# The last 64 tokens of four batches as one seven-product block instead of two pairs of full products

## The chip, the cores and the metric

The kernel runs on one core of a Trainium2 chip. The metric is the device time of one execution in microseconds (us). Before the change three executions took 236.12, 236.27 and 237.04 us; the median is 236.27 us. A core has a matrix engine (TensorE, PE in the profile; its weight loads are PEld), a vector engine (VectorE, DVE), an activation engine (ScalarE, ACT), a general engine (GpSimd, POOL) and a queue engine (SyncE, SP). Each works through its own instructions in order. SBUF is the on-chip memory, PSUM the accumulator of TensorE with 8 banks.

## The reference

Eight batches of 576 tokens and 8 heads go through an attention with 32 memory slots per head, and then through a gated feed-forward block:

```python
a = exp(phi - max(phi)); a = a / sum(a)                 # per token, over 32 slots
k_m = einsum('bhsm,bhsd->bhmd', a, k)
v_m = einsum('bhsm,bhsd->bhmd', a, v)
attn = softmax(q @ k_m.T / 8)                           # 576 x 32 per head
x = attn @ v_m                                          # tokens x 512
h = silu(x @ w_gate) * (x @ w_val)                      # 4608 x 1536
out = h @ w_out                                         # 4608 x 512
```

Only the last line is touched by the change: h (tokens x 1536) times w_out (1536 x 512). All of k, v and the products are in bfloat16 with float32 accumulation.

## The kernel before

h of a batch lies as `hts[b, c]`, 128 x 4 x 576, for three chunks c of 512 of the 1536 columns; the contraction runs over 128-row blocks. Of the 576 tokens, 512 are multiplied with w_out by a scheme with seven block products in place of eight (2 x 2 blocks: tokens halves times contraction pairs on one side, contraction pairs times output halves on the other). It needs sums of blocks of h (`Ss`) and of w_out (`Ts`), and adds results in VectorE when they leave PSUM. One product has six units, one unit two matmuls of 128x256 (u = 0, 1):

```python
def products(b, by_hand):
    ...
    def product(home, lhs, rhs, after):
        def unit(k):
            c, m = k // 2, k % 2
            def run():
                fresh = k == 0 and home not in mine
                if fresh:
                    mine[home] = bank([128, 2, h], FP32, f"p_o{home}")
                    ...
                for u in range(2):
                    nc.tensor.matmul(mine[home][:, u], lhsT=lhs(c, m, u), rhs=rhs(c, m),
                                     start=fresh and u == 0, stop=(k == 5), ...)
                if k == 5:
                    ...
                    if after in now:
                        now[after]()          # p1, q6, p5: ScalarE copies; c11, c12, c22: VectorE adds; c21: copy
    ...
    if b + 1 == B:
        return first + six + five + seven + three + four, ops
    return first + five + six + three + seven + four, ops
```

The adds write output tiles of which there are three in turn, and each is stored by queue transfers:

```python
work = ctx.enter_context(tc.tile_pool(name="work", bufs=3))
...
def add(out, home, other, free=False):
    nc.vector.tensor_tensor(out=out, in0=mine[home], in1=mine[other], op=ALU.add)
    ...
def c22():
    t = tile_of("o2", (128, 2, DM), tag="to")
    add(t[:, :, hi], "s", "p5")               # reads bank "s" after product seven
...
def c12():
    t = mine["o1"]
    add(t[:, :, hi], "c", "q6", True)
    both("o1", 0, ...)                        # the stores of o1
def c21():
    copy("v" if box.get("end") else "a", mine["o2"][:, :, lo], mine["s"])
    ...                                       # the stores of o2
```

Banks are called by their home: "s" takes products 1, 6, 7 and 4 one after the other (all accumulate; between them p1, q6 and c22 read it), "c" takes 5 and 3 (p5 reads it between them), "a" takes the second half of `first`.

The block sums of h are made as each chunk is done: on GpSimd for chunks 0 and 1, on VectorE for chunk 2. The remaining 64 tokens of each batch are copied by GpSimd into `xs`, two batches side by side (2 x 64 = 128 tokens), and multiplied in full, 12 contraction blocks for each half of the 512 output columns:

```python
def chunk_done(b, c):
    ...
    sums(nc.vector if end else nc.gpsimd)      # end: c == 2
    ...                                        # ends(): GpSimd copies the last 64 tokens into xs[b // 2]

def out_rest(pair, half):                      # 6 units of 2 matmuls 128x256
    ...
    for jf in (2 * n, 2 * n + 1):
        nc.tensor.matmul(mine["p"], lhsT=xs[pair][:, jf]..., rhs=WO[jf][:, cols],
                         start=(jf == 0), stop=(jf == NJF - 1))
    if n == NJF // 2 - 1:
        copy("v" if box.get("end") else "a", t_o, mine["p"])
        ...                                    # and two stores
```

The order is written by hand. For each batch b from 2: the products of batch b-1 wait in a backlog of units. Scores and softmax of batch b come between 36 of them; then 24 gate/value slots (each two matmuls for the gate p_g, silu on ScalarE into t_sg, two matmuls for the value p_v, a multiply on VectorE into t_h), with the rest of the backlog as fillers, the key/value sums of the next batch after eight slots (they use sums of exp(phi) that GpSimd makes first), and the weights of the next batch (`u_three`, six banks, four copies on ScalarE and two on VectorE) after twenty:

```python
for b in range(2, B):
    ...
        backlog += out_rest(b // 2 - 1, b % 2)
        run(take(6))
    if b > 2:
        loads(b)                              # GpSimd issues the loads of batch b + 2
    for g in range(NG):
        scores(b, g)
    ...                                       # z_inv_v, norm (t_A), 30 more units of the backlog
    if b == 2:
        u_three(2)
        run(out_rest(0, 0))
        u_values(2)
        backlog = one[36:]
    g = gv_slots(b)
    beside = 0 if last else min(7, len(backlog))
    outs = [lambda: run(take(1)) for _ in range(len(backlog) - beside)]
    streams = [(g, 0, 24), (outs, 4, 24)]
    ...
        (kv_items(b + 1, lambda: (u_item(b, 2, "aava")(), run(take(2)))), KV, KV + 4),     # KV = 7
        ([lambda: (run(take(2)), u_three(b + 1), run(take(3)))], 19, 20),
    spread(*streams)
    ...
run_late()
run(take(6))
ops["p1"]()
run(out_rest(B // 2 - 1, 0))
box["end"] = True                             # from here ScalarE issues half of the stores
run(take(6))
ops["c11"]()
run(backlog)
run(out_rest(B // 2 - 1, 1))
```

Of the kernel before, what the change touches and what calls it, by code (L numbers as in the profile page):

```python
# [14 lines left out]
def kernel(  # L15
# [52 lines left out]
    box = {}  # L68
# [516 lines left out]
    def chunk_done(b, c):  # L585
# [26 lines left out]
        if end and b > 1:  # L612
            late.append(ends)
        else:
            ends()
        if (b, c) in beside_sums:
            beside_sums[b, c]()

# [4 lines left out]
    }  # L623

# [10 lines left out]
    def store(t_o, b, t0, count, row=0, cols=slice(0, 512), queues=None):  # L635

        if queues is None and box.get("end"):
            queues = nc.sync, nc.scalar
        for n, (r0, m, bb, jj, pp) in enumerate(token_segments(b, t0, count)):
            eng = queues[n % len(queues)] if queues else nc.sync  # L640
            eng.dma_start(out=out_r[bb, jj, pp:pp + m, cols], in_=t_o[row + r0:row + r0 + m])

    def out_rest(pair, half):

        h = DM // 2
        mine = {}
        cols = slice(h * half, h * half + h)

        def unit(n):
            def run():  # L650
                if n == 0:
                    mine["p"] = bank([128, h], FP32, "p_oo")
                for jf in (2 * n, 2 * n + 1):
                    nc.tensor.matmul(  # L654
                        mine["p"],
                        lhsT=xs[pair][:, jf].rearrange("p a t -> p (a t)"),
                        rhs=WO[jf][:, cols],
                        start=(jf == 0),
                        stop=(jf == NJF - 1),
                    )  # L660
                if n == NJF // 2 - 1:
                    t_o = work.tile([128, h], FP32, tag="to", name="t_o")
                    copy("v" if box.get("end") else "a", t_o, mine["p"])
                    done(mine["p"])
                    end = 2 * pair + 2 == B
                    for k in range(2):
                        store(
                            t_o, 2 * pair + k, S - 64, 64, 64 * k, cols,
                            ((nc.sync, nc.scalar)[k],) if end else None,
                        )  # L670

            return run

        return [unit(n) for n in range(NJF // 2)]

    def products(b, by_hand):
# [3 lines left out]
        lo, hi = slice(0, h), slice(h, DM)  # L680

        def A(e, n):
            return lambda c, m, u: hts[b, c][
# [3 lines left out]
        def Sx(n):  # L687
            return lambda c, m, u: Ss[b, c][:, n, m, 128 * u:128 * u + 128]
# [7 lines left out]
# [4 lines that stand above are left out]
                def run():  # L700
                    fresh = k == 0 and home not in mine
                    if fresh:
                        mine[home] = bank([128, 2, h], FP32, f"p_o{home}")
                        mine[home, "new"] = True
                    for u in range(2):
# [17 lines left out]
        def tile_of(name, shape=(128, 2, h), **kw):  # L723
# [14 lines left out]
        def both(name, t0, cols):  # L738
            for u in range(2):
                store(mine[name][:, u, cols], b, t0 + 128 * u, 128, cols=cols)  # L740

        def c11():
            t = tile_of("o1", (128, 2, DM), tag="to")
            add(t[:, :, lo], "a", "p1", True)
            if box.get("end"):
                both("o1", 0, lo)

        def c22():
            t = tile_of("o2", (128, 2, DM), tag="to")
            add(t[:, :, hi], "s", "p5")  # L750
            if box.get("end"):
                both("o2", 256, hi)

        def c12():
            t = mine["o1"]
            add(t[:, :, hi], "c", "q6", True)
            both("o1", 0, hi if box.get("end") else slice(0, DM))

        def c21():
            t = mine["o2"]  # L760
            copy("v" if box.get("end") else "a", t[:, :, lo], mine["s"])
            done(mine["s"])
            both("o2", 256, lo if box.get("end") else slice(0, DM))
# [12 lines left out]
        if b + 1 == B:  # L776
# [177 lines left out]
    for b in range(2, B):  # L954
# [25 lines left out]
        else:  # L980
            backlog += out_rest(b // 2 - 1, b % 2)
# [23 lines left out]
        if b == 2:  # L1005
            u_three(2)
            run(out_rest(0, 0))
            u_values(2)
            backlog = one[36:]
        g = gv_slots(b)  # L1010
        beside = 0 if last else min(7, len(backlog))
        outs = [lambda: run(take(1)) for _ in range(len(backlog) - beside)]
        streams = [(g, 0, 24), (outs, 4, 24)]
# [53 lines left out]
```

The softmax here doesn't subtract the row's maximum and nothing guards it: scores larger than these inputs give would overflow.

## Time and profile before

| | |
|---|---|
| median of 3 runs | 236.27 us |
| span of the profiled run | 234.5 us, TensorE clock 1.00 |
| TensorE busy | 225.9 us, 2847 matmuls |
| VectorE, ScalarE, GpSimd busy | 187.4, 172.5, 135.2 us |
| gate and value matmuls p_g, p_v (L514) | 768 of 128x288 |
| leftover matmuls p_oo (L654) | 96 of 128x256 |
| block sums of h on GpSimd (L601, L559) | 68 of 128x512, 1155 to 1186 ns each |
| copies of the last 64 tokens (L591) | 24 |

The page of the profile lists an engine's busy time, the chain of work that ended last, and groups of equal instructions: line, engine, operation, output<-inputs, shape, count | busy us, mean ns of one | idle time of the engine before them and what ended it. [...]the durations of matmuls overlap; the distance of their starts is what each costs. A timeline line gives start, duration, engine, line, instruction, count, and in brackets the idle time before it with its releaser. SPq and ACTq are the issues of transfers by those engines.

### The profile page before, as it was taken

The page shows a single profiled execution, that of the slowest core. Times are in us where ns is not written, and L with a number is a line of the kernel's source. Part 1 is how long each engine was busy: PE and PEld are TensorE (multiplying, and loading weights), DVE is VectorE, ACT ScalarE, POOL GpSimd, SP SyncE. Part 2 cuts the span into 40 slices and gives each one's busy share as a digit, 9 for nine tenths or more (in the row PEclk, how much of TensorE's full clock was granted, in tenths as well). Part 3 has the DMA queues.
Part 4 walks back from the last instruction along what each step waited for, and adds up shares of the span by engine and source line. Part 5 has one row for each costly group of instructions (what it writes and reads, how often), then busy time and mean ns, then how long its engine had stood idle before and what let it go on. Part 6 is the DMA issues. An engine that isn't in the chain of part 4 may idle for free.

```text
span 234.5 us, 7300 instructions
## 1 busy us (share of the span) xinstructions
PE 225.9 (96%) x2847; PEld 171.3 (73%) x2847; DVE 187.4 (80%) x417; ACT 172.5 (74%) x368; POOL 135.2 (58%) x171
## 2 busy tenths in 40 slices
PE   7998899999999999999999999999999999999992
PEld 2555466778887777887778777877788777878881
DVE  4157699999979697998799878988799879987621
ACT  2758888988447888977898779968897789677310
POOL 8532426999099159654992399267916493029400
PEclk9999999999999999999999999999999999999999
DMA  6999999999974999899559964999313721122134
GB/s 211 205 205 207 198 208 206 228 238 248 207 169 97 252 216 158 166 247 232 137 80 252 214 110 106 225 226 142 110 25 81 132 89 27 31 62 89 33 92 126
DMA packets 42914, 36.84 MB, mean 157 GB/s; under 512 B 15488, under 2 KB 38528, under 8 KB 42880
## 3 DMA queue, kind: packets, MB, share of 16 engines
q0 software_dynamic: 21440, 22.42, 55.0%
q1 hardware_dynamic: 20176, 12.79, 25.8%
q10 hardware_dynamic: 1264, 1.18, 1.6%
q8 instruction: 22, 0.36, 0.6%
q14 instruction: 12, 0.10, 0.1%
HBM read 42.47 MB, written 9.44 MB: 221 GB/s over the span
## 4 chain that ended last, share of the span: by engine, by line
PE 82%; DMA 8%; POOL 4%; DVE 3%; issue 1%; ACT 0%; DVEq 0%; POOLq 0%
PE p_g L514 20%; PE p_v L514 19%; PE p_os L706 16%; PE p_oc L706 8%; DMA t_kv<-in_v_dram 8%; PE p_u L471 5%; PE p_oo L654 5%; PE p_oa L706 4%; PE p_kv L235 2%; POOL t_es L217 1%; POOL t_q L108 1%; PE p_g L400 1%; POOL t_kv L98 1%; DVE t_lz L443 1%; DVE t_z L434 1%
## 5 line engine op out<-in xcount | busy, mean ns | idle before, releaser
L537 DVE TENSOR_TENSOR t_h<-t_sg,p_v 128x288 bf16<-128x288 bf16 x192 | 83.1, 452 | 15.6 <-PE p_v L514 7.6
L514 PEld LDWEIGHTS <-t_U 128*128 128x128 bf16 x768 | 73.7, 98 | 21.7 <-issue 2.9
L531 ACT ACTIVATE t_sg<-p_g 128x288 bf16<-128x288 f32 x192 | 74.5, 423 | 15.9 <-PE p_g L514 9.1
L514 PE MATMUL p_g<-t_A,t_U 128*128 128x288 bf16 x384 | 77.2, 286 | 0.0
L514 PE MATMUL p_v<-t_A,t_U 128*128 128x288 bf16 x384 | 77.0, 286 | 0.0
L706 PEld LDWEIGHTS <-t_S 128*128 128x128 bf16 x384 | 37.4, 98 | 4.5 <-issue 0.2
L601 POOL TENSOR_TENSOR t_S<-t_h 128x512 bf16<-128x512 bf16 x17 | 19.7, 1156 | 35.2 <-DVE t_h L537 35.2
L491 ACT CAST t_U<-p_u 128x512 bf16<-128x512 f32 x53 | 28.0, 608 | 8.9 <-PE p_u L471 8.9
L706 PEld LDWEIGHTS <-t_h 128*128 128x128 bf16 x288 | 27.3, 98 | 7.8 <-issue 4.0
L706 PE MATMUL p_os<-t_T,t_S 128*128 128x256 bf16 x192 | 23.7, 273 | 0.0
L559 POOL TENSOR_TENSOR t_S<-t_S,t_h 128x512 bf16<-128x512 bf16 x17 | 19.6, 1155 | 1.3
L559 POOL TENSOR_TENSOR t_S<-t_h,t_S 128x512 bf16<-128x512 bf16 x17 | 20.1, 1186 | 0.0
L559 POOL TENSOR_TENSOR t_S<-t_h 128x512 bf16<-128x512 bf16 x17 | 19.6, 1155 | 0.0
L471 PE MATMUL p_u<-W,t_kT 64*32 64x512 bf16 (+1 forms) x416 | 15.9, 363 | 0.1
L706 PE MATMUL p_os<-t_T,t_h 128*128 128x256 bf16 x96 | 15.6, 273 | 0.0
L827 PE MATMUL p_warm<-bones 128*128 128x512 bf16 (+2 forms) x43 | 12.9, 427 | 1.7 <-DVE bones L850 1.7
L451 DVE TENSOR_TENSOR t_A<-t_E,t_lz 128x576 bf16<-128x576 bf16 x16 | 13.4, 840 | 0.9 <-ACT t_lz L427 0.3
L654 PE MATMUL p_oo<-WO,t_x 128*128 128x256 bf16 x96 | 14.0, 273 | 0.0
L495 DVE CAST t_U<-p_u 128x512 bf16<-128x512 f32 x19 | 12.4, 683 | 1.6 <-PE p_u L471 1.6
L215 POOL COPY t_mark<-t_A 1x1 bf16<-1x1 bf16 x4 | 0.7, 182 | 20.3 <-DVE t_A L451 20.3
L706 PE MATMUL p_oc<-t_T,t_S 128*128 128x256 bf16 x96 | 12.0, 273 | 0.0
L706 PE MATMUL p_oa<-WO,t_h 128*128 128x256 bf16 x96 | 11.8, 273 | 0.0
(93 smaller groups left out, 309.9 us busy)
## 6 DMA issues: line engine op xcount, KB each, us to landing
t_kv<-in_k_dram POOLq DMA_DIRECT2D x8, 576.0 KB, 10.1
t_kv<-in_v_dram POOLq DMA_DIRECT2D x8, 576.0 KB, 14.4
out_dram<-t_o SPq DMA_DIRECT2D x21, 192.0 KB, 2.6
t_phi<-in_phi_dram POOLq DMA_DIRECT2D x6, 576.0 KB, 7.9
t_q<-in_q_dram POOLq DMA_DIRECT2D x5, 576.0 KB, 7.4
out_dram<-t_o SPq DMA_DIRECT2D x37, 64.0 KB, 2.0
out_dram<-t_o SPq DMA_DIRECT2D x14, 128.0 KB, 5.8
t_q<-in_q_dram POOLq DMA_DIRECT2D x6, 288.0 KB, 11.3
```

Of the source, the lines that this page charges most:

```text
L451: nc.vector.tensor_tensor(out=a, in0=es.pop((b, g)), in1=lzs.pop((b, g)), op=ALU.mult)
L471: nc.tensor.matmul(p[g][32 * i:32 * i + 32, o:o + n], lhsT=kTs[b][64 * g:64 * g + 64, 2, 32 * i:32 * i + 32], rhs=w_part(w, c, i, g, halve ...
L491: nc.scalar.copy(out=t, in_=p)
L495: nc.vector.tensor_copy(out=t, in_=p)
L514: nc.tensor.matmul(p[:, 0:HALF], lhsT=Us[b, c, g][:, o // 2, which, 128 * (o % 2):128 * (o % 2 + 1)], rhs=atts[b, g][:, r], start=(g == 0) ...
L531: nc.scalar.activation(out=sg, in_=gate[:, 0:HALF], func=AF.Silu)
L537: nc.vector.tensor_tensor(out=dst, in0=sg, in1=val[:, 0:HALF], op=ALU.mult)
L559: eng.tensor_tensor(out=out, in0=x, in1=y, op=ALU.subtract)
L601: eng.tensor_tensor(out=t[:, 0], in0=A21, in1=A22, op=ALU.add)
L654: nc.tensor.matmul(mine["p"], lhsT=xs[pair][:, jf].rearrange("p a t -> p (a t)"), rhs=WO[jf][:, cols], start=(jf == 0), stop=(jf == NJF - 1),)
L706: nc.tensor.matmul(mine[home][:, u], lhsT=lhs(c, m, u), rhs=rhs(c, m), start=fresh and u == 0, stop=(k == 5), skip_group_check=u == 1 or n ...
L827: nc.tensor.matmul(p[:, 0:128 * a], lhsT=bones, rhs=x.to_broadcast([128, a, 128]) if a > 1 else bones, start=True, stop=True,)
```

## The change

Four batches have 4 x 64 = 256 leftover tokens: with the pair of batches as token halves, the same seven-product scheme fits, with a single matmul of 128x256 per unit in place of two. `products` gets a parameter `quad` for it: U = 1, the h blocks come from `xs[2 * quad]` and `xs[2 * quad + 1]`, and the block sums are made by GpSimd in `quad_sums`, four instructions of 128x256 for each chunk (one of them writes over a block in place). Quad 0 (batches 0 to 3) runs within the first six slots of batch 4. Quad 1 (batches 4 to 7) runs its first 12 units among the slots of batch 7 and the other 30 after everything else; there GpSimd waits by a small copy (t_mark) until the sums of VectorE for batch 7 are done. `out_rest` goes. With fewer units to spread, the counts of fillers beside other work are set anew (7 to 4, and 2 + 3 around `u_three` to 0 + 2), the fourth product of batch 1 takes the place of the leftover in batch 2, and the stores of the end alternate between the two queues by a running counter. The purpose is to save TensorE work: seven products instead of eight.

```diff
--- before.py
+++ after.py
@@ -613,14 +613,34 @@
             late.append(ends)
         else:
             ends()
+        if (b, c) in ((3, 0), (3, 1), (7, 0)):
+            quad_sums(b // 4, c)
         if (b, c) in beside_sums:
             beside_sums[b, c]()
+
+    Qs = {}
+
+    def quad_sums(qd, c):
+
+        x, y = xs[2 * qd], xs[2 * qd + 1]
+        t = att.tile([128, 3, 2, 128], BF16, tag=f"Q{c}", bufs=1, name="t_Q")
+        A11, A12, A21, A22 = (
+            z[:, 4 * c:4 * c + 4].rearrange("p (m e) a t -> p e m (a t)", e=2)[:, e]
+            for z in (x, y) for e in range(2)
+        )
+        nc.gpsimd.tensor_tensor(out=t[:, 0], in0=A21, in1=A22, op=ALU.add)
+        subtract(nc.gpsimd, t[:, 1], t[:, 0], A11)
+        subtract(nc.gpsimd, t[:, 2], A12, t[:, 1])
+        subtract(nc.gpsimd, A21, A11, A21)
+        Qs[qd, c] = t
 
     beside_sums = {
         (0, 0): lambda: (load_phi(3, nc.gpsimd), load_q_group(2, 0)),
         (1, 0): lambda: (load_q_group(2, 1), load_q(3)),
         (0, 1): lambda: (load_k(3), load_v(3)),
     }
+
+    turn = [1]
 
     def token_segments(b, t0, count):
         segs = []
@@ -636,55 +656,33 @@
 
         if queues is None and box.get("end"):
             queues = nc.sync, nc.scalar
-        for n, (r0, m, bb, jj, pp) in enumerate(token_segments(b, t0, count)):
-            eng = queues[n % len(queues)] if queues else nc.sync
+        for r0, m, bb, jj, pp in token_segments(b, t0, count):
+            eng = nc.sync
+            if queues:
+                turn[0] += 1
+                eng = queues[turn[0] % len(queues)]
             eng.dma_start(out=out_r[bb, jj, pp:pp + m, cols], in_=t_o[row + r0:row + r0 + m])
 
-    def out_rest(pair, half):
... (the whole function goes)
-    def products(b, by_hand):
+    def products(b, by_hand, quad=None):
 
         h = DM // 2
         mine = {}
         lo, hi = slice(0, h), slice(h, DM)
+        U = 2 if quad is None else 1
+        end = quad == 1 or (quad is None and b + 1 == B)
 
         def A(e, n):
+            if quad is not None:
+                return lambda c, m, u: xs[2 * quad + n][:, 4 * c + 2 * m + e].rearrange(
+                    "p a t -> p (a t)"
+                )
             return lambda c, m, u: hts[b, c][
                 :, 2 * m + e, 256 * n + 128 * u:256 * n + 128 * u + 128
             ]
 
         def Sx(n):
+            if quad is not None:
+                return A(0, 1) if n == 2 else lambda c, m, u: Qs[quad, c][:, min(n, 2), m]
             return lambda c, m, u: Ss[b, c][:, n, m, 128 * u:128 * u + 128]
 
         def W_(e, cols):
@@ -700,9 +698,9 @@
                 def run():
                     fresh = k == 0 and home not in mine
                     if fresh:
-                        mine[home] = bank([128, 2, h], FP32, f"p_o{home}")
+                        mine[home] = bank([128, U, h], FP32, f"p_o{home}")
                         mine[home, "new"] = True
-                    for u in range(2):
+                    for u in range(U):
                         nc.tensor.matmul(
                             mine[home][:, u],
                             lhsT=lhs(c, m, u),
@@ -720,7 +718,7 @@
 
             return [unit(k) for k in range(6)]
 
-        def tile_of(name, shape=(128, 2, h), **kw):
+        def tile_of(name, shape=(128, U, h), **kw):
             mine[name] = work.tile(list(shape), FP32, name=f"t_{name}", **kw)
             return mine[name]
 
@@ -736,31 +734,36 @@
                 done(mine[home])
 
         def both(name, t0, cols):
-            for u in range(2):
+            if quad is not None:
+                for k in range(2):
+                    x = 4 * quad + 2 * (t0 // 256) + k
+                    store(mine[name][:, 0, cols], x, S - 64, 64, 64 * k, cols)
+                return
+            for u in range(U):
                 store(mine[name][:, u, cols], b, t0 + 128 * u, 128, cols=cols)
 
... (c11, c22, c12, c21: tiles of U instead of 2, `end` instead of box.get("end"))
         ops = dict(
             p1=keep("p1", "s"), q6=keep("q6", "s"), p5=keep("p5", "c"),
@@ -773,7 +776,7 @@
         three = product("c", Sx(3), W_(1, hi), "c12")
         seven = product("s", Sx(2), T(2), "c22")
         four = product("s", A(1, 1), T(3), "c21")
-        if b + 1 == B:
+        if quad is None and b + 1 == B:
             return first + six + five + seven + three + four, ops
         return first + five + six + three + seven + four, ops
 
@@ -978,7 +981,6 @@
             backlog = one[6:12] + zero[36:] + one[12:36]
             ops = ops1
         else:
-            backlog += out_rest(b // 2 - 1, b % 2)
             run(take(6))
         if b > 2:
             loads(b)
@@ -1004,13 +1006,19 @@
         run(take(12))
         if b == 2:
             u_three(2)
-            run(out_rest(0, 0))
+            run(one[36:])
             u_values(2)
-            backlog = one[36:]
         g = gv_slots(b)
-        beside = 0 if last else min(7, len(backlog))
+        quad = []
+        if b == 4:
+            quad_sums(0, 2)
+            quad = products(b, (), 0)[0]
+        if last:
+            rest, rest_ops = products(b, (), 1)
+            backlog += rest[:12]
+        beside = 0 if last else min(4, len(backlog))
         outs = [lambda: run(take(1)) for _ in range(len(backlog) - beside)]
-        streams = [(g, 0, 24), (outs, 4, 24)]
+        streams = [(g, 0, 24), (quad, 0, 6), (outs, 6 if quad else 4, 24)]
         if last:
             streams += [([u_item(b, 2)], 5, 6)]
         if not last:
@@ -1021,21 +1029,24 @@
                 streams += [([lambda: loads(2)], 7, 8)]
             streams += [
                 (kv_items(b + 1, lambda: (u_item(b, 2, "aava")(), run(take(2)))), KV, KV + 4),
-                ([lambda: (run(take(2)), u_three(b + 1), run(take(3)))], 19, 20),
+                ([lambda: (u_three(b + 1), run(take(2)))], 19, 20),
             ]
         spread(*streams)
         flush_mul()
         units, ops = products(b, ("p1", "c11"))
         backlog += units
     run_late()
+    mark = att.tile([1, 1], BF16, tag="mark", bufs=1, name="t_mark")
+    nc.gpsimd.tensor_copy(out=mark, in_=Ss[B - 1, 2][0:1, 3, 0, 0:1])
+    for c in range(1, NCH):
+        quad_sums(1, c)
     run(take(6))
     ops["p1"]()
-    run(out_rest(B // 2 - 1, 0))
     box["end"] = True
     run(take(6))
     ops["c11"]()
     run(backlog)
-    run(out_rest(B // 2 - 1, 1))
+    run(rest[12:])
 # ---- launch: one core; inputs and outputs as the reference has them ----
 _INS = ['q', 'k', 'v', 'phi', 'moe_w_gate', 'moe_w_val', 'moe_w_out']
 _OUTS = [((4608, 512), 'float32')]
```

More of the change, by code (lines that the diff above doesn't have):

```diff
@@ L638, in store @@
             queues = nc.sync, nc.scalar
-        for n, (r0, m, bb, jj, pp) in enumerate(token_segments(b, t0, count)):
-            eng = queues[n % len(queues)] if queues else nc.sync
-            eng.dma_start(out=out_r[bb, jj, pp:pp + m, cols], in_=t_o[row + r0:row + r0 + m])
-    def out_rest(pair, half):
[L645 to L674, printed above, removed]
-    def products(b, by_hand):
+        for r0, m, bb, jj, pp in token_segments(b, t0, count):
[3 more added lines that the diff above has]
+                eng = queues[turn[0] % len(queues)]
+            eng.dma_start(out=out_r[bb, jj, pp:pp + m, cols], in_=t_o[row + r0:row + r0 + m])
+    def products(b, by_hand, quad=None):
         h = DM // 2
@@ L738, in both @@
         def both(name, t0, cols):
-            for u in range(2):
+            if quad is not None:
[4 more added lines that the diff above has]
+            for u in range(U):
                 store(mine[name][:, u, cols], b, t0 + 128 * u, 128, cols=cols)
         def c11():
-            t = tile_of("o1", (128, 2, DM), tag="to")
+            t = tile_of("o1", (128, U, DM), tag="to")
             add(t[:, :, lo], "a", "p1", True)
-            if box.get("end"):
+            if end:
                 both("o1", 0, lo)
         def c22():
-            t = tile_of("o2", (128, 2, DM), tag="to")
+            t = tile_of("o2", (128, U, DM), tag="to")
             add(t[:, :, hi], "s", "p5")
-            if box.get("end"):
+            if end:
                 both("o2", 256, hi)
@@ L756, in c12 @@
             add(t[:, :, hi], "c", "q6", True)
-            both("o1", 0, hi if box.get("end") else slice(0, DM))
+            both("o1", 0, hi if end else slice(0, DM))
         def c21():
             t = mine["o2"]
-            copy("v" if box.get("end") else "a", t[:, :, lo], mine["s"])
+            copy("v" if end else "a", t[:, :, lo], mine["s"])
             done(mine["s"])
-            both("o2", 256, lo if box.get("end") else slice(0, DM))
+            both("o2", 256, lo if end else slice(0, DM))
         ops = dict(
```

## The prediction

> **What bounds the kernel now.** I read the page first (busy shares, chain), then the chain in order of time, then stage sums and the timeline of one steady batch. The page says that TensorE is the limit, and the groups say what a leftover product is:
>
> ```profile
> PE 225.9 (96%) x2847; PEld 171.3 (73%) x2847; DVE 187.4 (80%) x417; ACT 172.5 (74%) x368; POOL 135.2 (58%) x171
> PE 82%; DMA 8%; POOL 4%; DVE 3%; issue 1%; ACT 0%; DVEq 0%; POOLq 0%
> L654 PE MATMUL p_oo<-WO,t_x 128*128 128x256 bf16 x96 | 14.0, 273 | 0.0
> ```
>
> The 273 ns are pipelined. The chain has the honest price: twelve in a row take 1.31 us, 0.109 us each.
>
> ```profile
> 219.68 1.31 PE p_oo L654 x12
> ```
>
> A batch lasts 25.25 us (windows between starts of the gate/value stretch: 102.0, 127.4, 152.6, 177.9, 203.2). I split it in three: (1) gate/value slots up to the large weight round (24 matmuls L471, "u_three"), 12.9 us; (2) the last four slots, 3.9 us; (3) scores, softmax and 36 units of output products, 8.5 us. "96% PE" hides that part 3 has a second engine at the limit. Stage sums of two such stretches (columns: PE, PEld, DVE, ACT, POOL busy, clock, DMA share, GB/s):
>
> ```profile
> 143.70:152.60 8.90, 8.90 (x101) 7.48 (x100) 8.50 (x17) 7.94 (x14) 4.15 (x8) 1.00 0.90 170
> 169.00:177.90 8.90, 8.90 (x101) 7.50 (x100) 8.50 (x17) 7.95 (x14) 1.37 (x4) 1.00 0.07 17
> ```
>
> VectorE is busy 8.50 of 8.90 us. The timeline from the weight round on shows it as one chain:
>
> ```profile
> 165.45 0.84 PE L471 MATMUL p_u<-W,t_kT 64*32 64x512 bf16 x24
> 165.93 2.05 ACT L491 CAST t_U<-p_u 128x512 bf16<-128x512 f32 x4 [0.58 <-PE p_u L471]
> 167.84 0.76 ACT L531 ACTIVATE t_sg<-p_g 128x288 bf16<-128x288 f32 x2
> 168.43 0.43 ACT L331 COPY t_o<-p_oo 128x256 f32<-128x256 f32 x1
> 168.33 1.83 DVE L537 TENSOR_TENSOR t_h<-t_sg,p_v 128x288 bf16<-128x288 bf16 x4 [0.22 <-ACT t_sg L531]
> 170.19 0.42 DVE L601 TENSOR_TENSOR t_S<-t_h 128x512 bf16<-128x512 bf16 x1
> ...
> 177.03 0.76 DVE L451 TENSOR_TENSOR t_A<-t_E,t_lz 128x576 bf16<-128x576 bf16 x1
> 177.86 0.41 PE L514 MATMUL p_g<-t_A,t_U 128*128 128x288 bf16 x2
> ```
>
> Weight round, four casts on ScalarE, last silus, last multiplies, four sums, softmax, last t_A at 177.79; TensorE starts the next batch at 177.86. From 165.45 on this chain of 12.4 us has under 0.2 us to spare. In batch 3 it is the longer one already (at 102 us t_A comes last).
>
> [...]t_A is 0.76 us alone and 1.29 when block sums run on GpSimd:
>
> ```profile
> 69.52 1.29 DVE L451 TENSOR_TENSOR t_A<-t_E,t_lz 128x576 bf16<-128x576 bf16 x1
> 69.04 2.78 POOL L559 TENSOR_TENSOR t_S<-t_h,t_S 128x512 bf16<-128x512 bf16 x2
> ```
>
> [...]four stores behind the softmax land 6.0 to 6.4 us after issue in batch 4, where the next loads are in flight, and after 2.0 to 2.6 in batch 6, which has none:
>
> ```profile
> DMA to landing us min/median/max: 6.0/6.1/6.4
> DMA to landing us min/median/max: 2.0/2.5/2.6
> ```
>
> **The change, part by part.**
>
> TensorE ledger. Out: 8 x 12 = 96 leftover matmuls. In: 2 quads x 7 products x 6 = 84 of the same shape. 12 x 0.109 = 1.31 us less. Batches 2, 3, 5, 6 lose 12 each; batch 4 gains 42 - 12 = 30; batch 7 stays (12 for 12); the tail has 30 for 24. So the gain is -1.31, if nothing else waits. I now go through what waits.
>
> a) Fillers behind the weight round. Of the six units taken from batches 3 to 6 (two matmuls, 0.22 us each), four lie in part 1, two behind the weight round. There the VectorE chain sets the time, so 2 x 0.22 = 0.44 us per batch is not gained. The chain itself hardly shrinks: by the instruction order, the 128x512 copy of the fourth product now stands on ScalarE between the four casts and the silus, where a 128x256 copy stood behind two of them. Four batches x 0.44 = +1.75.
>
> b) Batch 2. The fourth product of batch 1 now directly follows the weight round; it accumulates on the bank that an add on VectorE has still to read, and that add ends at 75.87 us, against 75.52 for the round: 0.4 us wait. +0.5 with what VectorE holds back.
>
> c) Token sums (GpSimd) before the key/value sums are on time to 0.1 us now (t_ehl ends at 131.24, TensorE uses it at 131.38); with one filler fewer before, 0.1 us each in three batches: +0.3.
>
> d) Block sums of the quads: 4 GpSimd instructions of 256 elements, 0.6 us each (128x256 f32 sums in L217: 1.26 us for two), 2.4 us a chunk. Two chunks come in batch 3, ahead of the sums of chunk 1 and of the loads. GpSimd was then done with its sums at 118.7 us; now it works 5 us longer, over the four S sums of VectorE (119.65 to 121.3) and perhaps the first t_A (123.23). [...]the milder form seen at 69.52 gives about 1.0; I take +2.0, all on the chain of part 3.
>
> e) The quad in batch 4. Its seventh product is followed at once by its fourth, on the same bank; between stands VectorE's add c22, whose output tile (three buffers) is that of the first output tile of batch 3. By the instruction order this add waits for four stores. They are issued 0.6 to 2.0 us after the last t_A; the loads, moved 5 us later by (d), are in flight; they land near 8.0 us. The add is wanted at 0.25 + 4 x 0.49 + 33 x 0.109 = 5.8 us. So TensorE stands from 5.8 to about 8.6 (add 0.4, hand-over 0.1): 2.8 us. Three units ahead of the first gate fill 0.33 us of the wait for t_A. +2.5.
>
> f) Tail. The quad's 30 matmuls follow the fourth product of batch 7. ScalarE both copies p5 of the quad and issues half of the stores, and stands still while it issues:
>
> ```profile
> 228.29 2.83 SPq L641 DMA_DIRECT2D out_dram<-t_o  x5
> 228.30 2.86 ACTq L641 DMA_DIRECT2D out_dram<-t_o  x5
> 228.88 0.69 DVE L333 COPY t_o<-p_os 128x512 f32<-128x512 f32 x1 [0.62 <-PE p_os L706]
> ```
>
> The copy on VectorE ends 0.72 us after the fourth product, two issues of 0.44 follow, p5 is copied from 1.65 to 2.0. The third product of the quad, ready at 1.31, waits for it: 0.7. Seventh to fourth again waits for c22: 0.16 drain + 0.42 + 0.05 = 0.6. +1.3. The last blocks' sums on GpSimd (5 us from about 223) are done before they are wanted at 227.7 to 230.
>
> Sum: -1.31 + 1.75 + 0.5 + 0.3 + 2.0 + 2.5 + 1.3 = +7.0, or 243.3 us. As (d) and (e) are taken near their full length, I put the middle at 242.6.
>
> **The rivals.** *The ledger alone holds:* 235.0. For it: PE at 96%, and windows in which it never idles. Against: VectorE's 8.50 of 8.90 and the 0.2 us of slack. *The quad's wait is short:* if the stores land by 5.8 us, (e) is 0.6 - 0.3, the sum +4.8, 241.1; for it: landings of 2.0 to 2.6 us without loads; against: here the loads come even later. *GpSimd becomes the bound:* if (d) [...]delays the loads until the softmax of a later batch waits for them, 246 or more; against: in batch 4 k and v for batch 6 have some 25 us in hand.
>
> **Range and chances.** Of the seven terms, the ledger, (a) and (f) rest on measured durations (+1.7 together); (d) can be 0.8 to 2.9, (e) 0.3 to 5 (stores behind all loads). That gives 239 to 246; I take 238.5 to 245.8, leaving room for waits that overlap. 2% slower is 241.0. Slower by over 2%: 0.70; within 2%: 0.27; faster by over 2%: 0.03, since the ledger has only 0.6% in it.
>
> **What would show it.** Right: TensorE idle or stretched by 2 to 3 us at one place in batch 4 (after some 5.8 us of its gate/value stretch), VectorE waiting there for DMA out_dram; S sums of VectorE before batch 4 longer than 0.42 us; softmax stretches with TensorE waiting 0.4 us for t_A; batches 5 and 6 of 24.5 us; a tail from the last value product to the end some 2 us longer. Wrong: no wait at c22 in batch 4, batches of 23.9 us, S sums of 0.42 us; then the ledger holds and the time is 235 to 237.

## The result and the profile after

The changed kernel takes 251.92 us (median of 6 runs, 250.62 to 253.08) against 236.81 us for the kernel before beside it: 1.064 times the time, 95% interval 1.0597 to 1.0683. It is slower, as predicted, but 9.3 us more so than the 242.6 us predicted, and outside the predicted range.

The page of the changed kernel, busy time and share of the span, the granted clock in 40 slices, and the chain by engine:

```profile
PE 228.7 (92%) x2835; PEld 171.2 (69%) x2835; DVE 191.9 (77%) x423; ACT 173.0 (69%) x368; POOL 152.4 (61%) x196
PEclk9999999999999999999999799999999999999999
PE 2%; DVE 1%; DMA 1%; ACTq 1%; ACT 0%; issue 0%
```

There are 12 matmuls fewer, as the ledger said, yet TensorE is busy 2.8 us longer, in a span of 249.0 us in place of 234.5. One slice has a lower clock; the kernel before had none. The chain (82% TensorE before) can be followed back only a few per cent from the end, through stores, so it says nothing of the middle. The view that does is that of the waits of TensorE (us in total, times, longest):

```profile
PE p_os L704 <- DVE t_o L732: 4.6, 3, 3.8
PE p_os L704 <- ACT t_q L727: 1.9, 1, 1.9
PE p_u L471 <- DMA t_kT<-t_bkv: 1.9, 1, 1.9
PE p_g L514 <- DVE t_A L451: 1.1, 1, 1.1
PE p_oc L704 <- ACT t_p L727: 1.1, 1, 1.1
```

In the kernel before TensorE never stood 0.4 us between two matmul starts after the first 40 us. Here the waits listed carry most of the loss (10.6 of 14.5 us). To see what each is worth I laid the starts of the stages of both traces side by side and took how much longer each stage lasts after than before:

| stage | longer by, us |
|---|---|
| batch 2, weight round to first gate (fourth product waits for c22) | +0.36 |
| batch 2, then up to the scores of batch 3 | -0.37 |
| batch 3, key/value sums to weight round (TensorE waits for the transpose t_kT) | +1.31 |
| batch 3, other stages | -0.4 |
| batch 4, weight round of batch 3 to first gate | +0.09 |
| batch 4, first gate to key/value sums (holds quad 0) | +10.75 |
| batch 4, then up to the first gate of batch 5 | -0.84 |
| batch 5, whole | +0.08 |
| batch 6, whole | -0.58 |
| batch 7, first to last gate product | +0.20 |
| tail | +4.02 |

(The rest, -0.1, is the start.) Two places hold it all: the gate stretch of batch 4, and the tail. I take the first apart. The timeline of VectorE and GpSimd before batch 4 (start, duration, engine, line, instruction):

```profile
120.62 0.74 DVE L601 TENSOR_TENSOR t_S<-t_h 128x512 bf16<-128x512 bf16 x1
...
122.62 0.88 DVE L559 TENSOR_TENSOR t_S<-t_h,t_S 128x512 bf16<-128x512 bf16 x1
...
124.00 0.66 POOL L559 TENSOR_TENSOR t_x<-t_x 128x256 bf16<-128x256 bf16 x1
...
125.34 0.97 DVE L451 TENSOR_TENSOR t_A<-t_E,t_lz 128x576 bf16<-128x576 bf16 x1
```

The S sums of VectorE, 0.41 to 0.50 us each before, take 0.74, 0.50, 0.89 and 0.88; GpSimd, done at 118.7 before, works until 124.66, and only then issues the loads. The first of them, in the kernel before and then in the changed one:

```profile
119.05 0.81 POOL L115 DMA_DIRECT2D t_q<-in_q_dram  x1
```

```profile
124.61 0.81 POOL L115 DMA_DIRECT2D t_q<-in_q_dram  x1
```

The second t_A is 1.3 us late: TensorE stands 1.28 us longer at the second gate product than it would. Then comes the stand at c22, in the timeline and, below, in sums of stretches (us; busy time of PE, PEld, DVE, ACT, POOL; clock; DMA share; GB/s):

```profile
134.70 0.71 PE L704 MATMUL p_os<-t_T,t_x 128*128 128x256 bf16 x5
138.74 0.42 DVE L732 TENSOR_TENSOR t_o<-p_os,t_p 128x256 f32<-128x256 f32 x1 [3.31 <-DMA out_dram<-t_o]
139.21 0.38 PE L704 MATMUL p_os<-t_T,t_x 128*128 128x256 bf16 x2 [3.81 <-DVE t_o L732]
```

```profile
135.00:139.20 4.20, 0.41 (x4) 0.21 (x3) 0.85 (x2) 0.06 (x1) 0.34 (x1) 1.00 1.21 223
139.20:141.00 1.80, 1.79 (x11) 1.33 (x11) 0.45 (x1) 0.41 (x1) 0.00 (x0) 0.65 1.26 196
141.00:143.00 2.00, 2.00 (x11) 1.28 (x9) 0.45 (x1) 1.18 (x3) 0.00 (x0) 0.50 1.10 241
```

TensorE is busy 0.41 of 4.20 us. The last matmul of the seventh product starts at 135.13, the fourth product at 139.21: a stand of 4.08 us, for VectorE's add, which waits for the stores of batch 3. After it the granted clock is 0.65 and then 0.50 until about 143. So the +10.75 are: 39 matmuls of the quad at 0.109 = 4.26 (the other three come ahead of the first gate); one filler unit less, -0.22; the wait for t_A, 1.28; the stand at c22 less one normal step, 3.97; together 9.3. What is left, about 1.5, falls in the stretch of the lower clock: 3.4 us at 0.50.

The tail, VectorE and ScalarE:

```profile
231.80 1.37 DVE L559 TENSOR_TENSOR t_S<-t_h 128x512 bf16<-128x512 bf16 x1
...
242.04 0.37 ACT L727 COPY t_p<-p_oc 128x256 f32<-128x256 f32 x1 [5.62 <-DMA out_dram<-t_o]
```

GpSimd's quad sums after chunk 0 of batch 7 (until 227.96) push its sums of chunk 1 onto the four S sums of VectorE, which now take 0.95, 1.26, 1.37 and 0.61. Batch 7's c11 comes late, ScalarE's store issues wait for it, and the copy q6 stands behind them: TensorE stands 2.19 us from 233.80. Then the copy p5 of the quad stands behind another six issues (a stand of 1.35 us), and c22 of the quad costs 0.79.

### The profile page after: what moved, and what is told of

It is laid out like the page before. It is cut to its first block, busy times and chain, and to the rows that moved or that the text cites. A ratio compares the mean times of both kernels' runs of the same rounds, so it can differ in the third digit from the quotient of the medians.

```text
span 249.0 us, 7306 instructions
## 1 busy us (share of the span) xinstructions
PE 228.7 (92%) x2835; PEld 171.2 (69%) x2835; DVE 191.9 (77%) x423; ACT 173.0 (69%) x368; POOL 152.4 (61%) x196
## 3 DMA queue, kind: packets, MB, share of 16 engines
q10 hardware_dynamic: 1344, 1.25, 1.6%
## 5 line engine op out<-in xcount | busy, mean ns | idle before, releaser
L537 DVE TENSOR_TENSOR t_h<-t_sg,p_v 128x288 bf16<-128x288 bf16 x192 | 82.1, 451 | 19.5 <-PE p_v L514 6.5
L531 ACT ACTIVATE t_sg<-p_g 128x288 bf16<-128x288 f32 x192 | 74.2, 422 | 24.5 <-PE p_g L514 17.4
L514 PE MATMUL p_g<-t_A,t_U 128*128 128x288 bf16 x384 | 78.4, 288 | 1.2 <-DVE t_A L451 1.1
L514 PE MATMUL p_v<-t_A,t_U 128*128 128x288 bf16 x384 | 78.0, 288 | 0.0
L704 PE MATMUL p_os<-t_T,t_h 128*128 128x256 bf16 x96 | 14.7, 274 | 0.3 <-DVE t_o L732 0.3
L591 POOL COPY t_x<-t_h 128x256 bf16<-128x256 bf16 x24 | 11.4, 480 | 0.9 <-DVE t_h L537 0.8
L732 DVE TENSOR_TENSOR t_o<-p_os,t_p 128x512 f32<-128x512 f32 (+1 forms) x10 | 6.3, 630 | 7.3 <-DMA out_dram<-t_o 3.3
## 6 DMA issues: line engine op xcount, KB each, us to landing
t_kv<-in_k_dram POOLq DMA_DIRECT2D x8, 576.0 KB, 10.5
```

The lines of the kernel that those rows point to most:

```text
L514: nc.tensor.matmul(p[:, 0:HALF], lhsT=Us[b, c, g][:, o // 2, which, 128 * (o % 2):128 * (o % 2 + 1)], rhs=atts[b, g][:, r], start=(g == 0) ...
L531: nc.scalar.activation(out=sg, in_=gate[:, 0:HALF], func=AF.Silu)
L537: nc.vector.tensor_tensor(out=dst, in0=sg, in1=val[:, 0:HALF], op=ALU.mult)
L591: nc.gpsimd.tensor_copy(out=xs[b // 2][:, 4 * c:4 * c + 4, b % 2], in_=hts[b, c][:, :, S - 64:S])
```

## The experiments

Theory: two causes in batch 4, each by itself: the block sums on GpSimd (my step d), and c22 on the stores (my step e); in the tail ScalarE's issues. The rivals: what is won at one place is lost at the next wait; the sums are hidden and it is the products' place that costs; TensorE's time is worth less than its count. All comparisons are against runs of the kernel before on the same chip (236.19 to 236.27 us median; 236.81 for the first row).

| run | us | ratio to before (95%) |
|---|---|---|
| changed kernel | 251.92 | 1.064 (1.060 to 1.068) |
| own result tiles for quad 0 | 246.92 | 1.046 (1.039 to 1.053) |
| end stores on one queue | 252.68 | 1.067 (1.062 to 1.073) |
| block sums late | 244.82 | 1.035 (1.030 to 1.041) |
| t_kT by TensorE | 251.00 | 1.060 (1.055 to 1.065) |
| own tiles + late sums | 242.97 | 1.028 (1.020 to 1.035) |
| the same + t_kT by TensorE + tail copies on VectorE | 241.25 | 1.019 (1.013 to 1.025) |
| the same + other order + fillers earlier | 241.39 | 1.022 (1.018 to 1.025) |
| the same, block sums left out | 239.75 | 1.013 (1.011 to 1.016) |
| before, leftover left out | 230.95 | 0.976 (0.970 to 0.982) |
| before + early sums | 245.01 | 1.036 (1.028 to 1.044) |
| before + late sums | 241.92 | 1.023 (1.021 to 1.026) |
| changed kernel, block sums left out | 244.75 | 1.035 (1.032 to 1.037) |

### Own result tiles for quad 0

Quad 0 adds and stores in the tiles of its copies p1 and p5, so that no tile in use by the stores of batch 3 is wanted.

```diff
 def c11():
-    t = tile_of("o1", (128, U, DM), tag="to")
+    t = mine["o1"] = mine["p1"] if quad == 0 else tile_of("o1", (128, U, DM), tag="to")
 def c22():
-    t = tile_of("o2", (128, U, DM), tag="to")
+    t = mine["o2"] = mine["p5"] if quad == 0 else tile_of("o2", (128, U, DM), tag="to")
```

> The changed kernel, but quad 0 writes its results into its own two tiles (those that keep p1 and p5) and no longer into one of the three output tiles. The add c22 of the quad then waits for no store. Store theory: the stand of TensorE in batch 4 (4.08 us between two matmuls in the changed kernel) falls to about 0.7 us, the low clock of the 3.8 us after it (0.65, 0.50) goes too: 3.4 + 1.1, so 4.5 us less, about 247.4 us. Rival, that the add stands behind other work of VectorE or that GpSimd's sums hold the quad: the gap stays above 2 us, the time within 1 us of 251.9.

Measured 246.92 us, 5.0 less. The waits of TensorE of this run have no 3.8 us for the add any more:

```profile
PE p_os L704 <- DVE t_o L736: 0.8, 2, 0.5
```

The stand at c22 falls from 4.08 to 0.79 us, and the clock stays at 1.00 afterwards; the gate stretch of batch 4 is 4.18 us shorter. So the wait is that for the output tile and its stores, and the lower clock is its consequence.

### The end's stores on one queue

```diff
-    queues = nc.sync, nc.scalar
+    queues = nc.sync, nc.sync
```

> The changed kernel, but at the end all stores go out on SyncE's queue, none on ScalarE's. If ScalarE's own issues hold its copies q6 and p5 (TensorE stands 2.08 and 1.24 us for them at the end): both gaps go, less about 0.5 us for stores in a row: about 2.8 us less, 249.1 us. Rival, that the late sums of VectorE hold the end by themselves: the first gap stays, less than 1 us gained or a loss.

Measured 252.68: no gain, a miss. The two stands for ScalarE's copies do go, so they were due to the stores that it issues. But now every store of the end stands in one queue (an issue there took 0.41 us in the kernel before, median of its last seven), and c22 of quad 1 waits for stores; VectorE in this run's tail:

```profile
243.43 0.42 DVE L732 TENSOR_TENSOR t_o<-p_os,t_p 128x256 f32<-128x256 f32 x1 [2.43 <-DMA out_dram<-t_o]
```

TensorE stands 3.06 us there from 240.85 on: the same kind of wait as in batch 4, in place of the two removed.

### The block sums late

The sums of quad 0's first two chunks follow the loads of batch 4, and those of quad 1's first chunk follow VectorE's S sums.

```diff
-        if (b, c) in ((3, 0), (3, 1), (7, 0)):
-            quad_sums(b // 4, c)
 ...
             loads(b)
+        if b == 4:
+            quad_sums(0, 0)
+            quad_sums(0, 1)
 ...
-    for c in range(1, NCH):
+    for c in range(NCH):
         quad_sums(1, c)
```

> The changed kernel, but GpSimd makes the block sums of chunks 0 and 1 of quad 0 after it has issued the loads of batch 4, and those of chunk 0 of quad 1 after the mark at the end: nothing of the quads stands any more ahead of the block sums of chunk 1 and of the loads. [...]the four S sums of VectorE before batch 4 and at the end fall from 0.50 to 1.37 us to 0.42 to 0.50, the last t_A before batch 4 comes 1.3 to 1.6 us earlier, the wait for q6 at the end (2.08 us) goes; with loads 5 us earlier the stores land sooner and the 4.08 us gap falls to 3 or less: 4 to 5 us less, about 247.5 us. Rival, that it is only the order of products and queues: S sums shorter, but less than 1.5 us gained.

Measured 244.82, 7.1 less: more than expected. Three things follow from this one edit: the wait for t_A in batch 4 goes; the stand at c22 is 2.21 in place of 4.08 us, since the loads are at their old time again and the four stores that it waits for land 5.0 to 5.5 us after their issue in place of 5.9 to 7.1, and no lower clock follows; and the tail's stand at q6 goes (the tail is 2.06 shorter).

### The transposes by TensorE

```diff
 def kv_T(b):
-    if b > 3:
+    if b > 7:
         nc.sync.dma_start_transpose(out=kTs[b], ...)
```

> The changed kernel, but the transposes of the key/value means go through TensorE (3 matmuls, a 0.35 us copy) in all batches, not through a DMA from batch 4 on. TensorE stands 2.07 us in batch 3 and 0.77 us in batch 5 ahead of the large weight round for t_kT from the DMA. If that DMA sets the time there: 2 to 2.5 us less, about 249.6 us. Rival, that the VectorE chain behind the round has the same length anyhow or that what is gained is waited for at the next DMA (t_qT): less than 1 us.

Measured 251.00, the rival's case. The stage of batch 3 with the wait for t_kT is 1.80 shorter, and the gate stretch of batch 4 is 1.78 longer. Of that, 1.13 is the wait for t_A (2.52 us between two matmul starts in place of 1.39); most of the rest goes with a clock of 0.50 for 6.8 us in place of 3.4. The wait, in the view of waits:

```profile
PE p_g L514 <- DVE t_A L451: 2.2, 1, 2.2
```

TensorE arrived earlier and only waited longer: this stand for VectorE's t_A ends at 129.45 us, and at 129.56 in the changed kernel. The 1.80 us gained ahead of the softmax were worth nothing here, where that chain ends last.

### Own tiles and late sums; then more repairs

The first two edits that helped, together:

> The changed kernel with both repairs: quad 0 has its own result tiles (no wait for the stores of batch 3), and the block sums of the quads on GpSimd come after the loads of batch 4 and, for the last quad, after the sums of VectorE. Theory A (two separate causes, store wait and GpSimd sums ahead of VectorE's sums): with the late sums alone (244.8) a stand of 2.2 us at c22 was left; own tiles cut it to about 0.7, so 1.5 less, 243.3 us (242.6 to 244.0). Rival B (what is freed is given back at the next wait for a DMA transpose, as with the TensorE transposes): 244.5 or more, with longer waits for t_kT in batches 3 and 4.

Measured 242.97: theory A (243.3), not the rival. Then t_kT by TensorE, and the copies p5 and q6 of the last quad on VectorE:

```diff
-    nc.scalar.copy(out=tile_of(name, tag=name, bufs=1), in_=mine[home])
+    copy("v" if quad == 1 and box.get("end") else "a", tile_of(name, tag=name, bufs=1), mine[home])
```

> As the kernel with both repairs, and also: the transposes of k for the weight rounds by TensorE in all batches instead of by DMA from batch 4 on, and the copies p5 and q6 of the last quad by VectorE instead of ScalarE, which issues stores then. Theory A: the waits for t_kT go (2.2 us in batch 3, about 0.9 in batch 5, with 0.1 to 0.4 of transposes added each) and the tail loses the 1.3 us before the third product: 240 to 241 us. Rival B: the chain of VectorE and ScalarE takes it back before the next gate stretch as in the run with the TensorE transposes alone (t_A wait of 2.5 us in batch 4): 242 to 243.3, only the tail's 1.2 us stays.

Measured 241.25, just above theory A's 240 to 241. With the GpSimd chain out of the way the stage of batch 3 that waited for t_kT keeps 1.25 of its gain; but 0.63 of that is lost again in batch 4's gate stretch, where TensorE now stands 0.51 us for t_A, and the tail is only 0.5 us shorter: there is a new stand of 0.44 us for ScalarE's copy q6 of batch 7, behind two store issues that took 1.29 us here and 0.98 in the run before.

### The most that TensorE's time is worth

The kernel before without its leftover products, their copies and stores (the last 64 tokens of each batch are not computed):

```diff
-    for jf in (2 * n, 2 * n + 1):
+    for jf in ():
 ...
-    if n == NJF // 2 - 1:
+    if False:                        # no copy, no stores
```

> The kernel before with its leftover products left out altogether: 96 matmuls, their copies and their stores (the output lacks the last 64 tokens of each batch). This is the upper limit of what any scheme for the leftovers can save. If TensorE's time were the bound everywhere: 96 x 0.109 = 10.5 us less, 225.8 us. By the theory of the prediction (from the weight round to the next gate stretch VectorE's chain sets the time; two to four of six units of a batch lie there): the tail's 2.6 us count in full, of the other 7.9 about half: 229 to 231 us. If new waits for DMA or GpSimd appear: above 231.

Measured 230.95, 5.2 us less for 10.5 us of matmuls: half. Sums over batch 4, from about its first gate product to that of batch 5, for the kernel before and then for this run (us; busy time of PE, PEld, DVE, ACT, POOL; clock; DMA share; GB/s):

```profile
127.40:152.60 25.20, 25.20 (x332) 19.88 (x331) 22.12 (x48) 20.88 (x45) 16.66 (x23) 1.00 0.87 167
```

```profile
126.24:150.68 24.44, 24.31 (x321) 18.74 (x319) 21.52 (x48) 20.60 (x44) 16.74 (x22) 1.00 0.83 164
```

Twelve matmuls out of the batch (1.31 us) shorten it by 0.8 us. In batch 5 they give nothing (25.27 us for 25.30): its weight round waits 0.9 us for t_kT. The tail, whose 2.6 us were expected in full, is 1.42 us shorter. The half is thus a sum of different waits, and holds for this order of the work. TensorE still shows 24.31 of 24.44 us busy: "busy" at 99% in the matmul's modelled durations does not mean that a matmul removed is a matmul gained.

### The block sums by themselves

The kernel before with the GpSimd sums of quad 0 and of quad 1's first chunk where the changed kernel makes them, their results unused.

```diff
+        if (b, c) in ((3, 0), (3, 1), (7, 0)):
+            quad_sums(b // 4, c)             # t_Q only, nothing reads it
 ...
+        if b == 4:
+            quad_sums(0, 2)
```

> The kernel before, with the block sums of the quads added on GpSimd where the changed kernel makes them (after chunks 0 and 1 of batch 3, at the gate stretch of batch 4, after chunk 0 of batch 7), their results unused; all products stay. This takes step (d) by itself. Prediction's (d): +2.0 us (0.8 to 2.9) before batch 4, S sums of VectorE there longer than 0.42 us; total 237.8 to 239.5 with up to 0.5 in the tail. Rival: in the changed kernel the wait came from the other order of TensorE, and the sums alone are hidden: within 0.5 us of before, 236.7 or less. If the loads, issued 5 us later, also cost (t_kT later in the next batch): above 239.5.

Measured 245.01: 8.8 us more than before, over four times the +2.0 of my step (d), with all products as before. The waits of TensorE in this run:

```profile
PE p_oo L668 <- POOL t_x L591: 2.7, 1, 2.7
PE p_kv L263 <- POOL t_ehl L223: 2.2, 1, 2.2
PE p_g L514 <- DVE t_A L451: 1.7, 1, 1.7
```

Only the third is what step (d) spoke of. The other two are waits for GpSimd itself. GpSimd's timeline in batch 4:

```profile
131.25 0.67 POOL L559 TENSOR_TENSOR t_Q<-t_x 128x256 bf16<-128x256 bf16 x1
131.87 0.18 POOL L215 COPY t_mark<-t_A 1x1 bf16<-1x1 bf16 x1
132.01 1.15 POOL L217 TENSOR_TENSOR t_es<-t_ephi 128x512 f32<-128x512 bf16 x1
```

The token sums begin at 132.01 (127.38 before), behind the quad sums of chunk 2, and the key/value sums on TensorE need their result. In the tail the copies of the last 64 tokens come behind the sums of chunk 1, which come behind the quad sums. S sums of VectorE in this run: 0.98, 1.26, 0.61, 0.89 us, together 2.0 us longer than before, as much as I had foreseen for them.

The late sums alone (quad 0 only), after the loads of batch 4:

> The kernel before with the block sums of quad 0 added on GpSimd, results unused, now after the loads of batch 4 (those of the last quad left out). GpSimd then starts its token sums for the next batch 2.7 us later: the wait of TensorE at the key/value sums is about 2.7 us, the S sums of VectorE stay near 0.42 us, up to 0.5 more at t_A: 238.7 to 239.7 us, against 242.4 for the early sums without their 2.6 us in the tail. Rival (GpSimd's time itself is what counts, wherever it stands): 242 or more.

Measured 241.92: 5.7 us, between theory and rival. The first S sum is at its old length, and the wait is where I expected it, but the clock was not foreseen. A wait of TensorE, the two stretches from 132 us on, and a sum of VectorE, each from its own view of this run:

```profile
PE p_kv L263 <- POOL t_ehl L223: 2.6, 1, 2.6
```

```profile
132.00:136.00 4.00, 1.05 (x9) 0.56 (x7) 1.08 (x3) 0.82 (x2) 3.50 (x7) 0.98 1.18 193
136.00:140.00 4.00, 4.00 (x101) 2.62 (x102) 1.96 (x7) 2.00 (x5) 0.00 (x0) 0.59 0.39 87
```

```profile
120.73 0.42 DVE L601 TENSOR_TENSOR t_S<-t_h 128x512 bf16<-128x512 bf16 x1
```

By stages: +3.56 up to the key/value sums (2.91 of it the stand), +1.31 in the following stage with the clock at 0.59, and +1.18 for t_kT in batch 3, before anything was changed: that transpose lands 3.6 us after its issue in the profiled run of before, 4.4 here and 3.9 with the early sums. So a wait for t_kT in batch 3 appears also where no edit comes before it; why is not shown, and I do not put all of it down to the change.

### The products by themselves

The changed kernel without block sums (the quads multiply blocks of h as they are; the last 64 tokens come out as other numbers).

```diff
 def Sx(n):
     if quad is not None:
-        return A(0, 1) if n == 2 else lambda c, m, u: Qs[quad, c][:, min(n, 2), m]
+        return A(n % 2, n // 2)
 def quad_sums(qd, c):
+    return
```

> The other half of the sums-alone run: the changed kernel without any block sums of the quads (its products multiply blocks of h as they are, so the last 64 tokens come out as other numbers). If the costs of the sums (8.8 us alone) and of the products simply add up, 251.9 - 8.8 = 243.1 us. If they hide each other in part (TensorE is late anyway where the key/value sums wait for GpSimd), the products alone cost more than that: 244 to 245 us, as with the late sums (244.8), with the stand of some 2 us at c22 for the stores. By the prediction without its step (d): 243.3 - 2.0 = 241.3.

Measured 244.75. With this the parts can be set against each other:

| | no block sums | early | late |
|---|---|---|---|
| products of before | 236.3 | 245.0 (+8.8) | 241.9 (+5.7, quad 0 only) |
| products of the quads | 244.75 (+8.5) | 251.9 (+15.1) | 244.8 (+8.6) |

Early sums and products all but add up (17.3 against 15.1); the match is loose, since 2.9 us of the early sums alone is a stand at leftover products (p_oo) that the changed kernel does not have. Late sums and products do not: 5.7 + 8.5 would be 14.2, and 8.6 is measured. The late sums make TensorE wait for t_ehl, and exactly there the quad has 4.3 us of other matmuls for it: with its products and late sums there is no such stand in batch 4. In the run of the products alone the stand at c22 is 2.63 us and the clock after it 0.63, 0.50, 0.50, 0.67 in four stretches of 1 us.

### The best version, and its floor

All repairs, the order six, five, seven, three, four in the quads and in batch 1, and the two fillers of a batch ahead of the key/value sums:

```diff
-        if quad is None and b + 1 == B:
+        if quad is not None or b + 1 == B or b == 1:
             return first + six + five + seven + three + four, ops
 ...
-        streams = [(g, 0, 24), (quad, 0, 6), (outs, 6 if quad else 4, 24)]
+        streams = [(g, 0, 24), (quad, 0, 6), (outs, 6 if quad else 2, 24 if last else 7)]
```

> The best of the repairs together: as the kernel with own tiles, late sums, TensorE transposes and tail copies on VectorE (241.25), and also: in the quads and in batch 1 the third product between the seventh and the fourth, so that c22 is done before its bank is wanted, and the two fillers of each batch before the key/value sums instead of spread over all slots. Theory: 0.7 at c22 in batch 4, 0.7 in the tail, 0.4 in batch 2, 0.2 in each of two batches less: 239.0 to 239.6 us, still above before, since batch 4 has 30 matmuls more and the other batches give back less than what was taken from them. Rival (waits only move on): 240.5 or more. A version that beats before would need below 236.

Measured 241.39, the rival's case: the waits for c22 and t_ehl go, and the waits of TensorE show two others in their place:

```profile
PE p_os L702 <- POOL t_Q L559: 1.5, 1, 1.5
PE p_os L702 <- POOL t_S L559: 0.8, 2, 0.5
```

Without the stand at c22 TensorE meets the late quad sums (1.82 us in batch 4), and ahead of batch 2's weight round the seventh product, moved forward, meets GpSimd's sums of batch 1. The same version without the block sums:

> The best version with the block sums of the quads left out (last 64 tokens come out as other numbers): what the saving is worth when GpSimd's part costs nothing. By the ledger 12 matmuls less would be 235.0. By the theory (half of what is taken from batches 2, 3, 5, 6 lies beside other waits, all 30 added in batch 4 count): 48 out are worth about 2.6 us, 30 in batch 4 cost 3.3 to 4.6, 6 in the tail 0.65: 238 to 239 us, within 0.7 of the best version with sums.

Measured 239.75, 0.75 above what I expected of it, and still 1.3% (1.1 to 1.6) above before. The gate stretch of batch 4 is 4.41 us longer, almost the full 4.47 of the 41 matmuls that it has more; batches 5 and 6, 12 matmuls (1.31 us) poorer each (and 3 transposes richer), are only 0.63 and 0.75 us shorter; batches 2 and 3 together give nothing; the tail costs 1.02. None of the versions with the quads beats the kernel before. All of them have quad 0 in the first six slots of batch 4; another place for it was not tried.

## Why the prediction was right and wrong

The direction and both main places were right; the size was not.

**Ledger, -1.31.** The count is right (2835 matmuls for 2847). (The gate stretch of batch 3 starts at 101.69 us before, not at 102.0 as I read it; no term rests on that.) What went wrong is its use: what is taken from batches 2, 3, 5 and 6 does not come back in full, what is put into batch 4 and the tail costs in full.

**(a), +1.75.** Too large: from the weight round to the next gate stretch 0.24 us per batch was gained where I expected nothing. **(c), +0.3,** was too small by about as much: TensorE stands 0.5 us for t_ehl in batches 5 and 6 where 0.1 was allowed. Together they leave batch 6 at 24.72 us, against 24.5 predicted (25.38 for batch 5, which also waits 0.9 us for t_kT). That only half of the removed matmul time is won is shown by the run without the leftover.

**(b), +0.5.** Right: a stand of 0.68 us, stage +0.36.

**(d), +2.0.** This is the step that failed. That VectorE's S sums last longer beside GpSimd's sums was right: they take up to 0.89 us before batch 4 and 1.37 in the tail, against 0.41 to 0.51 at the same places before. How much longer was my estimate, and I counted only the part on VectorE before batch 4. In the changed kernel that part is 1.28 us at t_A. Not counted was that GpSimd's other work comes later too: the loads, so that the stores of batch 3 land later (stand at c22 4.08 instead of 2.63 us), and in the last batch the block sums of chunk 1, pushed onto VectorE's by the quad's sums of chunk 0, which make the tail 2.1 us longer (4.02 against 1.94 without block sums); the prediction took only the quad's last sums into account there ("done before they are wanted"). Measured: a ratio of 1.064 with the sums and 1.035 without, about 7 us in place of 2.0. The two profiled runs differ by 5.7 us: 1.3 at t_A, 1.4 at c22, 2.1 in the tail, 0.7 for t_kT in batch 5, the rest in small parts. The size of one instruction was off too, 0.67 us for 0.6.

**(e), +2.5.** The wait, its place and its releaser were as predicted, 2.63 us without the block sums against 2.8 predicted. Missing were the extra 1.45 us from (d), and the lower clock after the stand: in the run of products alone the stage is 8.21 us longer, of which 4.26 - 0.22 + 2.52 = 6.56 are counted work and wait, and about 1.6 is left for the clock.

**(f), +1.3,** and 0.65 for six more matmuls: the places were right, and the sum came out by luck. The tail is 1.94 us longer with the products alone (predicted 1.95); but the stand for p5 is 1.33 us between starts and not 0.7, and what follows the last matmul is 0.63 us shorter (4.01 for 4.64), which I did not have. What the changed kernel loses beyond that is (d).

**Not seen at all:** the waits for DMA transposes. In batch 3 the stage to the weight round should have lost 0.65 us by the ledger and is 1.31 longer with t_kT landing last, and at the scores of batch 3 TensorE stands 1.01 us for t_qT, 0.9 more than a normal step: that is the 0.94 us by which batch 2 falls short of the ledger. A wait for t_kT appears without the change too, as the run with late sums alone showed; how much of it belongs to the change stays open.

So: without block sums I predicted +5.0 and measured +8.5. By the profiled run the surplus is 1.5 in batch 3 (t_kT), 0.9 in batch 2 (t_qT), 1.0 in batch 4 (the clock, less small gains) and 0.6 in batches 5 to 7, less 0.4 elsewhere. For the block sums I predicted +2.0 and measured about +7. The rival "GpSimd becomes the bound: 246 or more", which I set aside because k and v had 25 us in hand, was the nearest; I looked at when the loads are used, and not enough at the stores that are in flight with them (5.9 to 7.1 us to landing, against 5.0 to 5.5 with the loads at their old time) nor at what stands behind the sums in GpSimd's order.

## What to carry to other kernels

Work put on a half idle engine is not free: list everything that stands behind it in that engine's order (loads, copies, sums for a later stage) and give each its own term, and place it where another engine has work of its own to hide it, as the late sums beside the quad's products were hidden for 5.6 of 14.2 us. Before saving matmuls, measure what they are worth by leaving them out: here the whole leftover, 10.5 us of matmuls, was worth 5.2 us; an eighth of that is 0.65 us (an estimate), and with all 24 block sums left out the best version was still 3.5 us slower than before. A long stand of TensorE can cost twice, by itself (4.08 us in the changed kernel) and by the lower clock behind it (0.50 for 3.41 us, about 1.5 us of time).

## What was not expected of the hardware

The granted clock falls at stands much shorter than I had thought of. With stands of 2.63 us (products alone), 2.91 (late sums alone), 4.08 (changed kernel) and 4.26 (end stores on one queue) it was 0.50 for about 3.4 us, and for about 6.8 us with one of 4.24 (t_kT by TensorE). After stands of 2.18 and 2.19 us (changed kernel), 2.37 (late sums), 2.44 (early sums alone) and 2.52 (t_kT by TensorE) it stayed at 1.00, and once after 2.94 us too, in the tail with the early sums alone. So the length of a stand does not decide by itself, as 2.63 us had a low clock behind them and 2.94 us had none. The fall and the rise in the changed kernel, as sums of stretches (us; busy time of PE, PEld, DVE, ACT, POOL; clock; DMA share; GB/s):

```profile
136.34:139.75 3.41, 0.54 (x5) 0.46 (x5) 0.42 (x1) 0.00 (x0) 0.00 (x0) 1.00 1.22 198
139.76:143.16 3.40, 3.40 (x33) 2.30 (x39) 0.92 (x3) 1.60 (x4) 0.00 (x0) 0.50 1.16 225
143.17:248.98 105.81, 97.27 (x1172) 76.02 (x1156) 82.38 (x173) 71.54 (x156) 59.77 (x75) 1.00 0.43 90
```

The clock falls at 139.76, 0.55 us after the stand has ended (139.21), and is back at 1.00 at 143.17. In the 3.41 us ahead of that fall TensorE stood 2.87 us. In the runs of the products alone and of the late sums alone the falls are at about 136.45 and 135.85, 0.26 and 0.42 us after their stands have ended; there the whole stands, 2.63 and 2.91 us, lie in the 3.41 us ahead of the fall. What sets the moment of the fall, and why the 2.94 us had no effect, is not shown, and no run moved a stand to test it.

VectorE's S sums and GpSimd's block sums last longer beside each other: in the tail of the changed kernel GpSimd's took 1.16 to 1.34 us (1.15 alone), and S sums that took 0.41 to 0.51 us before took 0.95, 1.26, 1.37 and 0.61, so that the four lasted 4.1 in place of 1.7 us. Why is not shown.
